# A fused attention and MLP kernel: forward substitution for two groups per instruction, with two layout changes by way of DRAM

## The chip, the cores and the metric

The kernel runs on one core of a Trainium2 chip. The core has a matrix engine (TensorE, PE in the profile), a vector engine (VectorE, DVE), an activation engine (ScalarE, ACT), a general engine (GpSimd, POOL), a sequencer that issues the transfers here (SyncE, SP), and 16 DMA engines between DRAM and the on-chip memory. The metric is the device time of one execution in microseconds (us). The profile is one execution of its own.

## The reference

Three blocks follow each other; the first is a linear attention with a delta rule, the others are MLP blocks. Only the first is touched.

```python
k_n = k / (np.linalg.norm(k, axis=-1, keepdims=True) + 1e-06)
for t in range(S):                       # B, H, S, D = 4, 8, 768, 48
    y[:, :, t] = q[:, :, t] @ state                       # per (b, h)
    v_old = state.T @ k_n[:, :, t]
    state = state + beta[:, :, t] * outer(k_n[:, :, t], v[:, :, t] - v_old)
x = y as (B, S, H * D)                   # 768 tokens of 384 features per batch
x = first MLP(x): gelu(x @ w_in), spatial gate over the tokens, @ w_out, residual
x = second MLP(x): token mixing, then channel mixing, each with a residual
```

## The kernel before

The loop over 768 tokens is cut into chunks of 64 tokens. Inside a chunk the recurrence is a triangular system: with the Gram matrix of the chunk's keys (K Kᵀ), scaled by beta and the norms, its inverse turns values into updates. A 64 x 64 inverse is built from two 32 x 32 blocks, each by forward substitution, and one product that joins them.

The work is staged in **six groups** (two batch pairs, three thirds of the sequence). One group holds 32 blocks of 32 x 32 per 32-row partition quarter. For each group there is a *preparation* and then a *chain*.

The preparation of a group, `prep(g)`:

- Gram blocks: four units of 32 matmuls from Kᵀ (`kq`), each copied out of PSUM by ScalarE in six pieces (L145 to `Md`, L146 to `G`).
- A VectorE transpose of all 32 x 32 blocks (L151) puts the block number on the partitions: `Li`. Then norms and scaling (L155 to L170; L166 scales `Li`).
- The forward substitution: 31 steps. Step j multiplies row j of `Li` with column j of the growing inverse `T` into a scratch tile `p` (L191) and adds it to `T` (L193). A step is split by rows of `T`: rows 0 to 3 and 4 to 11 are two VectorE instructions, the rest one GpSimd instruction, so a step of a late j is six instructions. Every add waits for its product, and every product for the last add.
- Five more VectorE transposes: four (L197) bring the inverse back into the matmul layout `tw`, one (L201) makes `Tn`.
- `merge`: four rounds of 64 small matmuls, each with a ScalarE copy (L209 to L221), join the two halves. `wt`: four units of 32 matmuls with a ScalarE copy (L229, L232).

The masked product of queries and keys, `qk(g)`, has four units; each is masked on VectorE when it leaves PSUM (L128). Gram, `merge`, `wt` and `qk` outputs share two PSUM buffers (`gm`).

The chain of a group, `chain(g)`, goes through its four chunks in 16 *positions*, four per chunk: updates (`ck`, L270), state (`Sps`, L256), outputs (`yp`, L246). It is serial from chunk to chunk. While chain g runs, pieces of later groups are put between its positions by a table (`act`): the preparation of group g+1 is finished, that of group g+2 is begun. So each engine's queue is a fixed order written out by the program; an instruction that waits holds back what is behind it on its engine. SP issues all transfers, in that order too. Dummy matmuls (`wm`, L300) are put between positions to keep PE busy.

Beside chains 0 to 2, the weights `w_in` (64-bit floats) are converted on VectorE, ScalarE and GpSimd in 12 pieces (tile `F`, L413 to L418), and stored to DRAM (`scr`). Beside chain 5 the MLP blocks begin; they run until the end.

## Time and profile before

| | us |
|---|---|
| median of 3 runs (lowest, highest) | 1008.41 (1006.48, 1009.87) |
| span of the profiled execution | 1010.4 |
| PE busy | 889.8 (88 %) |
| DVE busy | 660.8 (65 %) |
| ACT busy | 425.5 (42 %) |
| POOL busy | 317.1 (31 %) |
| DMA | 60.99 MB, mean 60 GB/s |

The profiled execution is 2.0 us longer than the median of the runs. The busy times are unions over the whole span; the attention (up to about 369 us) and the MLP blocks (from about 326 us) have different limits, and must be read apart. A line such as `L191 DVE ... x348 | 87.7, 285 | 1.1` is a group of instructions: 348 of them, 87.7 us busy together, 285 ns on average, and 1.1 us that the engine sat idle just before them. In the table by windows each engine has its busy time and, in brackets, its instructions; then come the granted PE clock (1.00 is full), the share of the 16 DMA engines that was busy, and GB/s. In the timeline the columns are start and duration in us.

### The profile page before, as it was taken

What the parts mean: (1) busy time and instruction counts of PE and PEld (TensorE: products, weight loads), DVE (VectorE), ACT (ScalarE), POOL (GpSimd) and SP (SyncE); (2) the same over time, 40 slices, a digit from 0 to 9 for tenths busy, and PEclk for the clock granted to TensorE, in tenths of its full rate; (3) what the DMA queues carried; (4) which work ended last, traced back from release to release, by engine and by line L of the source; (5) the groups of instructions that cost most, each with busy time, mean ns of one, the idle gap of its engine ahead of it and who ended that gap; (6) DMA issues with size and microseconds to landing.
All of it is one profiled execution on the core that took longest, in us unless ns stands there. A gap on an engine that the chain in (4) does not pass through costs nothing.

```text
span 1010.4 us, 23691 instructions
## 1 busy us (share of the span) xinstructions
PE 889.8 (88%) x9764; PEld 819.7 (81%) x9764; DVE 660.8 (65%) x1612; ACT 425.5 (42%) x1029; POOL 317.1 (31%) x475
## 2 busy tenths in 40 slices
...
GB/s 371 130 49 1 69 127 159 180 57 121 35 75 38 139 125 64 1 1 1 1 2 1 1 72 66 94 63 111 67 24 25 1 24 24 1 24 24 1 25 23
DMA packets 28955, 60.99 MB, mean 60 GB/s; under 512 B 3760, under 2 KB 9904, under 8 KB 28080
## 3 DMA queue, kind: packets, MB, share of 16 engines
...
q14 instruction: 31, 0.25, 0.1%
...
## 4 chain that ended last, share of the span: by engine, by line
PE 59%; DVE 28%; ACT 7%; issue 4%; POOL 1%; DVEq 0%; POOLq 0%; ACTq 0%
PE ps L489 18%; PE ps L490 18%; PE ps L491 18%; DVE p L191 6%; DVE T L193 6%; DVE tw L197 3%; DVE F L413 2%; DVE aq L128 2%; DVE F L414 2%; PE wm L300 1%; PE ps L513 1%; DVE F L415 1%; DVE F L418 1%; ACT Md L145 1%; DVE Li L151 1%
## 5 line engine op out<-in xcount | busy, mean ns | idle before, releaser
L581 DVE SCALAR_TENSOR_TENSOR hlo<-ps,hh 128x384 fp32r<-128x384 f32 x96 | 53.5, 557 | 208.9 <-ACT hh L580 208.9
L580 ACT ACTIVATE hh<-ps 128x384 fp32r<-128x384 f32 x96 | 47.2, 492 | 229.8 <-PE ps L491 229.8
L489 PE MATMUL ps<-GU,SB 128*128 128x384 f32 x288 | 98.7, 343 | 0.0
L491 PE MATMUL ps<-GU,SB 128*128 128x384 f32 x288 | 98.4, 342 | 0.0
L490 PE MATMUL ps<-GU,SB 128*128 128x384 f32 x288 | 98.1, 341 | 0.0
L191 DVE TENSOR_TENSOR p<-Li,T 128x31 f32<-128x31 f32 (+28 forms) x348 | 87.7, 285 | 1.1
L193 DVE TENSOR_TENSOR T<-T,p 128x31 f32<-128x31 f32 (+28 forms) x348 | 84.1, 274 | 0.8
L490 PE MATMUL ps<-SB,VHt 128*128 128x384 f32 x192 | 65.8, 343 | 2.3 <-POOL SB L391 2.3
L491 PE MATMUL ps<-VHt,hlo 128*128 128x384 f32 x192 | 65.3, 340 | 1.3 <-DVE hlo L581 1.3
L300 PE MATMUL wm<-dum 128*128 128x512 bf16 x156 | 51.5, 436 | 16.4 <-DVE dum L319 14.8
L489 PE MATMUL ps<-SB,VHt 128*128 128x384 f32 x192 | 65.6, 341 | 0.0
L491 PE MATMUL ps<-SB,VHt 128*128 128x384 f32 x192 | 65.2, 339 | 0.0
L489 PE MATMUL ps<-VHt,hh 128*128 128x384 f32 x192 | 65.0, 338 | 0.0
L490 PE MATMUL ps<-VHt,hh 128*128 128x384 f32 x192 | 64.6, 337 | 0.0
L556 POOL TENSOR_TENSOR q<-q,u 128x384 f32<-128x384 f32 x32 | 36.9, 1159 | 66.5 <-DVE q L555 66.5
L489 PE MATMUL ps<-X,SA 128*128 128x384 f32 x144 | 50.0, 347 | 7.2 <-DVE xn L568 3.2
L490 PEld LDWEIGHTS ps<-GU,SB 128*128 128x128 f32 x288 | 54.9, 191 | 0.6 <-DVE GU L506 0.6
L489 PEld LDWEIGHTS ps<-GU,SB 128*128 128x128 f32 x288 | 55.0, 191 | 0.5 <-DVE GU L506 0.5
L491 PEld LDWEIGHTS ps<-GU,SB 128*128 128x128 f32 x288 | 54.8, 190 | 0.3 <-POOL SB L391 0.3
L191 POOL TENSOR_TENSOR p<-Li,T 128x19 f32<-128x19 f32 (+19 forms) x115 | 41.4, 360 | 35.2 <-DVE T L168 27.1
L229 PE MATMUL gm<-tw,kn 128*48 128x64 f32 x768 | 30.2, 245 | 23.9 <-DVE aq L128 19.7
L490 PE MATMUL ps<-X,SA 128*128 128x384 f32 x144 | 49.3, 343 | 0.0
...
## 6 DMA issues: line engine op xcount, KB each, us to landing
...
v<-in_vn_dram SPq DMA_DIRECT2D x12, 384.0 KB, 4.2
...
aq<-in_qt_dram SPq DMA_DIRECT2D x8, 512.0 KB, 7.7
...
```

Source lines behind the costliest of these rows:

```text
L128: else: nc.vector.tensor_tensor(aq[rr,par].rearrange("p a c x -> p (a c) x"),gp[rr],mask[rr].rearrange("p t x -> p (t x)").unsqueeze(1).to ...
L191: e.tensor_tensor(p,Li[:,j,j+1:].unsqueeze(1).to_broadcast([128,w,n]),T[:,a:a+w,j].unsqueeze(2).to_broadcast([128,w,n]),ALU.mult)
L193: e.tensor_tensor(T[:,a:a+w,j+1:],T[:,a:a+w,j+1:],p,ALU.add)
L197: nc.vector.transpose(out=tw[rr,q//2,:,co:co+32].rearrange("p n i -> p i n"),in_=T[rr].rearrange("p c i -> p i c"))
L229: nc.tensor.matmul(wt[D_[par],2*pair+cc,:],KNs[pb][F_[par],bb,par,2*h+cc,pair,:],tw[F_[par],par,16*bb+8*h+2*pair+cc,:],start=True,stop=True)
L300: for i in range(n): nc.tensor.matmul(t,dum[:,0:128],dum,start=True,stop=True)
L489: nc.tensor.matmul(ps,L[0],Rr[0],start=first,stop=False)
L490: nc.tensor.matmul(ps,L[0],Rr[1],start=False,stop=False)
L491: nc.tensor.matmul(ps,L[1],Rr[0],start=False,stop=last)
L556: nc.gpsimd.tensor_tensor(gt,gt,u2[:,d,t],ALU.mult)
L580: nc.scalar.activation(hi,ps,AF.Relu)
L581: nc.vector.scalar_tensor_tensor(lo,ps,0.0,R(hi),op0=ALU.max,op1=ALU.subtract)
```

## The change

1. **Substitution.** From group 1 on, groups are solved in pairs, (1,2), (3,4) and then (5) alone. `T` and `Li` have a leading index for the two groups, and a step is two VectorE instructions, one product and one add, over both groups and all rows. GpSimd no longer takes part. Group 0 is solved as before.
2. **Gram blocks to `Li` by DRAM.** From group 1 on, ScalarE copies a whole Gram unit at once (`gf`) and SP stores it to a DRAM tile `gd`. Function `li` reads it back as `Li`, in four transfers per group of 32 x 32 runs of 128 bytes each. The lower-left blocks (`G`) are read from `gd` too (`gload`: two such transfers). The VectorE transpose to `Li` is gone for these groups.
3. **Inverses by DRAM.** `T` is stored to a DRAM tile `td`, and `tload` reads it back into `tw`, in four transfers of 32 x 32 runs of 128 bytes. The four VectorE transposes per group are gone; the one to `Tn` stays.
4. **Kᵀ in quarters.** Instead of two whole tiles there are four tiles of one unit. A list (`_jobs`) gives the order of use by Gram and `qk` units; each use issues the load for the fourth use after it. Kᵀ is so read twice per group. The zero halves of `kq`, `aq` and `kn` are set by memsets at the start and no longer loaded.
5. **Order.** The table `act` has a row per group. Its letters: S a step of the substitution sequence (`li`, three preparatory steps, 31 steps, the stores and `Tn`), K a Gram unit, Q a `qk` unit, t `tload`, G `gload`, m a `merge` or `wt` unit, z the zeroing of `tw`, l and x the load and scaling of V, v the first values, c a step of the weight conversion. No dummy matmuls stand between the positions of a chain any more. All four `qk` units of group 0 are masked on VectorE.

```diff
-        KQs=[P1.tile([128,2,2,2,544],F32,name=f"kq{i}") for i in range(2)]
+        KQs=[P1.tile([128,2,512],F32,name=f"kq{i}") for i in range(4)]
+        GD=[PD.tile([128,32,64],F32,name=f"gd{g}") for g in range(6)]
+        TD=[PD.tile([128,32,32],F32,name=f"td{g}") for g in range(6)]
+        def load_kq():
+            kind,g,u=jobs[put[0]]; bp,sc=groups[g]; kq=KQs[put[0]%4]; put[0]+=1
+            for par in range(2):
+                nc.sync.dma_start(kq[H_[par],par],I['kq'][bp,sc][H_[par],u//2,u%2])
...
+        def kk(g):
...
+                    gf=P2.tile([128,8,64],F32,name="gf")
+                    nc.scalar.copy(gf,gp)
+                    nc.sync.dma_start(GD[g][:,u0:u0+8,:],gf)
...
+        def li(gs):
+            for s,g in enumerate(gs):
+                for q in range(4):
+                    r=slice(32*q,32*q+32); co=32*(q%2)
+                    nc.sync.dma_start(Li[r,s],GD[g][r,:,co:co+32].rearrange("i n j -> n i j"))
+                if g>0: nc.sync.dma_start(BT[gs[0]%2][:,s],I['bt'][groups[g]])
...
-            sets=[((nc.vector,nc.gpsimd)[e],a,b_) for e,a,b_ in ((0,0,d0),(0,d0,bd),(1,bd,32)) if a<b_]
+            if g0==0:
+                sets=[((nc.vector,nc.gpsimd)[e],a,b_) for e,a,b_ in ((0,0,d0),(0,d0,bd),(1,bd,32)) if a<b_]
+            else: sets=[(nc.vector,0,32)]
...
-                    e.tensor_tensor(p,Li[:,j,j+1:].unsqueeze(1).to_broadcast([128,w,n]),T[:,a:a+w,j].unsqueeze(2).to_broadcast([128,w,n]),ALU.mult)
+                    e.tensor_tensor(p,Li[:,S,j,j+1:].unsqueeze(2).to_broadcast(for_),T[:,S,a:a+w,j].unsqueeze(3).to_broadcast(for_),ALU.mult)
-                    e.tensor_tensor(T[:,a:a+w,j+1:],T[:,a:a+w,j+1:],p,ALU.add)
+                    e.tensor_tensor(T[:,S,a:a+w,j+1:],T[:,S,a:a+w,j+1:],p,ALU.add)
...
+                for s,g in enumerate(gs): nc.sync.dma_start(TD[g],T[:,s])
+                for s,g in enumerate(gs):
+                    nc.vector.transpose(out=TN[g%2].rearrange("p n c -> p c n"),in_=T[:,s])
+        def tload(g):
+            for q in range(4):
+                rr=slice(32*q,32*q+32); co=32*(q%2)
+                nc.sync.dma_start(tw[rr,q//2,:,co:co+32],TD[g][rr].rearrange("n c i -> c n i"))
+        def gload(g):
+            for q in (0,2):
+                nc.sync.dma_start(G21s[g%2][rr],GD[g][rr,:,32:64])
...
+        S=seqs(solve((1,2)),later((3,4)),later((5,)))
...
+ACT=[['S2','S2 Q','S2 K','S2','S2 Q K','S2 K','S2 K','S2 Q','S K','Q K t G l','K','K','m c x','m c','m2 c','m4 v'],
+     ['z S','S','t G S c','S','S','Q S2','m S2','Q S2','m S2','l Q S2 m K','S2 m K','Q S2 m K','S2 m K x','S2 m','S2 m','S2 v'],
+     ['z S2','S2','S2 c2','S2','S2 c2','Q S2','Q c2','S4 t G','Q','l Q','S','m','m x','m2','m2','m2 v'],
+     ['z S','S','t G','S','Q S2','S2','Q S2','m S2','Q m S2','l m S2','Q m S2','m S2','m S2 x','m S2','m S2','S4 v'],
+     ['z S3','S3','S3','S6 t G','Q','','Q','','Q m','l m','Q m','m','m x','m','m2','v']]
```

How the orders differ, at the three places on which the prediction rests.

VectorE, before: from the last step of group 0's substitution into the preparation of group 1 (`tw` is the inverse in the matmul layout, `Md` the Gram blocks).

```order
L193 TENSOR_TENSOR T<-T,p_635 128x7
L197 STREAM_TRANSPOSE tw_98<-T 32x32x32 x2
L201 STREAM_TRANSPOSE Tn<-T 128x32x32
L197 STREAM_TRANSPOSE tw_98<-T 32x32x32 x2
L151 STREAM_TRANSPOSE Li<-Md 128x1024
L158 TENSOR_SCALAR rc<-sh 128x32
```

VectorE, now: the same place. The two masks of group 0's first `qk` unit stand where the transpose to `Li` stood; then the preparatory steps have 64 columns, and each step of the substitution is one product and one add over both groups, with the later `qk` masks between them.

```order
L209 STREAM_TRANSPOSE tw_100<-T 32x32x32 x2
L128 TENSOR_TENSOR aq_98<-gm,mask 64x512 x2
L172 TENSOR_SCALAR rc<-sh 128x64
...
L201 TENSOR_TENSOR p_174<-Li,T 128x120
L203 TENSOR_TENSOR T<-T,p_174 128x2x2x30
L128 TENSOR_TENSOR aq_98<-gm,mask 64x512 x2
L201 TENSOR_TENSOR p_174<-Li,T 128x174
L203 TENSOR_TENSOR T<-T,p_174 128x2x3x29
```

So nothing on VectorE waited for a transfer there before; now L172 and all behind it stand behind the eight transfers to `Li`.

SP, now: from the end of chain 0 into chain 1. The loads for group 2 (`kn`, `aq`) wait until chain 0 has read its own; behind them stand `Li` of groups 3 and 4, and behind that `tw` and `G` of group 2.

```order
L87 DMA kn_102<-in_kn_dram 64x2x768 x2
L77 DMA aq_98<-in_qt_dram 64x4x512 x2
L159 DMA Li<-gd_121 32x32x32 x4
L160 DMA bt_143<-in_bt_dram 128x32
L159 DMA Li<-gd_122 32x32x32 x4
L160 DMA bt_143<-in_bt_dram 128x32
L226 DMA tw_100<-td_126 32x32x32 x4
L230 DMA G_148<-gd_120 32x32x32 x2
```

SP, before, at the corresponding place (`kq` is Kᵀ, `st` a piece of the weights):

```order
L76 DMA kq_111<-in_kq_dram 64x4x544 x2
L77 DMA bt<-in_bt_dram 128x32
L96 DMA kn_100<-in_kn_dram 64x2x768 x2
L84 DMA aq_96<-in_qt_dram 64x4x512 x2
L402 DMA st<-in_win_dram 128x512 x2
```

Before, SP only brought operands in; now the substitution and the merges of coming groups wait behind these transfers, which go in the order shown.

More of the change, by code (lines that the diff above doesn't have):

```diff
@@ L129, in qk @@
-                yield 'qk'
-        def prep(g):
-            pb=g%2; tw=TWs[pb]
-            Md=P1.tile([128,32,32],F32,name="Md")
-            G21=Gs[g%2]
-            for h in range(2):
-              for bb in range(2):
-                kq=KQs[g%2][:,h,bb]
+                    nc.vector.tensor_tensor(aq[rr,par].rearrange("p a c x -> p (a c) x"),gp[rr],mask[rr].rearrange("p t x -> p (t x)").unsqueeze(1).to_broadcast([64,8,64]),ALU.mult)
+                yield 'qk'
+        def kk(g):
+            Md=TN[0]
+            for u in range(4):
+                h,bb=u//2,u%2; u0=16*bb+8*h
+                kq=take_kq('k',g,u)
@@ L147, in prep @@
-                yield 'kk'
-            Li=P1.tile([128,32,32],F32,name="Li")
-            T=P1.tile([128,32,32],F32,name="T"); TL[0]=T
-            nc.gpsimd.memset(T,0.0)
-            nc.vector.transpose(out=Li,in_=Md.rearrange("p n i -> p i n"))
+                        c_=kq[F_,par,64*n:64*n+64]
+                        nc.tensor.matmul(gp[T_[par],n],c_,c_,start=True,stop=True)
+                load_kq()
+                if g==0:
+                    for r in range(4):
+                        q=slice(32*r,32*r+32)
+                        nc.scalar.copy(Md[q,u0:u0+8,:],gp[q,:,32*(r%2):32*(r%2)+32])
+                        if r%2==0: nc.scalar.copy(G21s[0][q,u0:u0+8,:],gp[q,:,32:64])
+                else:
+                    gf=P2.tile([128,8,64],F32,name="gf")
+                    nc.scalar.copy(gf,gp)
+                    nc.sync.dma_start(GD[g][:,u0:u0+8,:],gf)
@@ new lines, in kk, with solve @@
+                done[g]+=1
+                yield 'kk'
+        done=[0]*6
+        def li(gs):
+            assert all(done[g]==4 for g in gs)
+            for s,g in enumerate(gs):
[3 more added lines that the diff above has]
+                if g>0: nc.sync.dma_start(BT[gs[0]%2][:,s],I['bt'][groups[g]])
+        def solve(gs):
+            m=len(gs); S=slice(0,m); g0=gs[0]; BTs=BT[g0%2]
+            if g0>0: nc.gpsimd.memset(T[:,S],0.0)
+            else: nc.vector.transpose(out=Li[:,0],in_=TN[0].rearrange("p n i -> p i n"))
+            Lf=Li.rearrange("p s i j -> p s (i j)"); Tf=T.rearrange("p s i j -> p s (i j)")
+            n2=Lf[:,S,0:1024:33]
+            nt=lambda n_:P2.tile([128,2,32],F32,name=n_)[:,S]
+            sh,s1,rc,nr,bi,rr2,nn=[nt(x) for x in ('sh','s1','rc','nr','bi','rr2','nn')]
+            nc.scalar.activation(sh,n2,AF.Sqrt)
@@ L255, in ds @@
                     for par in range(2):
-                        nc.tensor.matmul(Sps[bb][D_[par],pair,:],KNs[pb][F_[par],bb,par,c,pair,:],yr[F_[par],pair,par,:],start=(gc==0 and pair==0 and bb==0),stop=True,skip_group_check=True)
+                        nc.tensor.matmul(Sps[bb][D_[par],pair,:],KNs[pb][F_,bb,par,c,pair,:],yr[F_,pair,par,:],start=(gc==0 and pair==0 and bb==0),stop=True,skip_group_check=True)
                 for par in range(2):
```

286 lines of the change are left out of this document (137 added, 149 removed).

## The prediction

> **What bounds the kernel now.** First the page: span, busy times, and the chain of work that ended last, by engine.
>
> ```profile
> span 1010.4 us, 23691 instructions
> PE 889.8 (88%) x9764; PEld 819.7 (81%) x9764; DVE 660.8 (65%) x1612; ACT 425.5 (42%) x1029; POOL 317.1 (31%) x475
> PE 59%; DVE 28%; ACT 7%; issue 4%; POOL 1%; DVEq 0%; POOLq 0%; ACTq 0%
> ```
>
> PE ends most of the chain, but that is an average over two halves. The view by windows separates them.
>
> ```profile
> core 0: us, PE busy (x) PEld busy (x) DVE busy (x) ACT busy (x) POOL busy (x), PEclk, DMA share, GB/s
> 62.00:112.00 50.00, 35.32 (x817) 27.01 (x815) 48.61 (x158) 31.81 (x84) 22.62 (x49) 0.84 0.12 27
> 160.00:217.00 57.00, 39.27 (x939) 33.62 (x939) 56.02 (x164) 33.08 (x92) 30.28 (x59) 0.85 0.48 129
> 270.00:320.00 50.00, 40.00 (x1172) 34.38 (x1164) 38.74 (x117) 32.30 (x84) 22.53 (x42) 0.97 0.29 72
> 730.00:1010.40 280.40, 276.61 (x1587) 274.83 (x1586) 68.83 (x127) 49.01 (x103) 0.00 (x0) 1.00 0.05 18
> ```
>
> In the attention VectorE is busy 97 to 98% of the time; only beside chain 4, with no substitution left, does it fall to 77%. At the end PE alone bounds, and nothing there changes. So I ask one thing: when does chain 5 start? All behind it keeps its length. The timeline of PE gives the first `ck` of chains 0, 1, 2, 3, 4 and 5:
>
> ```profile
> 70.97 0.32 PE L270 MATMUL ck<-yr,tw 128*64 128x48 f32 x2 [2.40 <-ACT yr L238]
> 131.98 0.34 PE L270 MATMUL ck<-yr,tw 128*64 128x48 f32 x1
> 191.72 0.26 PE L270 MATMUL ck<-yr,tw 128*64 128x48 f32 x1
> 243.80 0.34 PE L270 MATMUL ck<-yr,tw 128*64 128x48 f32 x1
> 290.88 0.26 PE L270 MATMUL ck<-yr,tw 128*64 128x48 f32 x1
> 325.88 0.26 PE L270 MATMUL ck<-yr,tw 128*64 128x48 f32 x1
> ```
>
> Chain 5 starts at 325.9. The distances are 61, 60, 52, 47 and 35 us; the last one is what a chain costs when VectorE has almost no substitution.
>
> **What goes.** The groups, by line:
>
> ```profile
> L191 DVE TENSOR_TENSOR p<-Li,T 128x31 f32<-128x31 f32 (+28 forms) x348 | 87.7, 285 | 1.1
> L193 DVE TENSOR_TENSOR T<-T,p 128x31 f32<-128x31 f32 (+28 forms) x348 | 84.1, 274 | 0.8
> L197 DVE STREAM_TRANSPOSE tw<-T 32x1024 f32<-32x1024 f32 x24 | 47.3, 1971 | 0.9
> L201 DVE STREAM_TRANSPOSE Tn<-T 128x1024 f32<-128x1024 f32 x6 | 11.9, 1990 | 0.2
> L128 DVE TENSOR_TENSOR aq<-gm,mask 64x512 f32<-64x512 f32 x40 | 27.6, 689 | 15.0 <-PE gm L121 14.1
> ```
>
> Substitution costs (87.7 + 84.1)/6 = 28.6 us of VectorE per group, the four transposes 7.9. For the new steps I need the price of one dependent instruction with GpSimd silent:
>
> ```profile
> 107.72 0.19 DVE L191 TENSOR_TENSOR p<-Li,T 128x31 f32<-128x31 f32 x1
> 107.95 0.19 DVE L193 TENSOR_TENSOR T<-T,p 128x31 f32<-128x31 f32 x1
> 109.38 0.28 DVE L191 TENSOR_TENSOR p<-Li,T 128x112 f32<-128x112 f32 x1
> 109.69 0.27 DVE L193 TENSOR_TENSOR T<-T,p 128x112 f32<-128x112 f32 x1
> ```
>
> Start to start 0.23 us at 31 elements and 0.31 at 112: 1.0 ns per element and 0.19 fixed. A step j of a pair has 2(j+1)(31-j) elements; over 31 steps, product and add, that is 21,824. So a pair takes 62 x 0.19 + 21.8 x 1.04 = 34 us, 17 per group instead of 28.6. With the transposes, VectorE loses about 20 of its 50 us per group. It no longer bounds a chain by its sum.
>
> **What comes.** Each `li`, `tload` or `gload` transfer has 1,024 runs of 128 bytes, 64 on each DMA engine. Between two chains' starts stand 6 of them, and 8 more (4 for group 5) where a pair is fetched. No row has such a transfer. Two stretches show small packets, the first with 16-byte rows (`gh`), the second mostly with 128-byte rows (`bt`) at the tail of a Kᵀ load:
>
> ```profile
> DMA packets 142, 0.00 MB, mean 5 GB/s; under 512 B 142, under 2 KB 142, under 8 KB 142
> q1 hardware_dynamic: 142, 0.00, 17.5%
> DMA packets 77, 0.02 MB, mean 56 GB/s; under 512 B 70, under 2 KB 70, under 8 KB 77
> q1 hardware_dynamic: 77, 0.02, 40.1%
> ```
>
> Both windows are 0.4 us of 16 engines, 6.4 us. The first gives 1.12 us/142 = 8 ns per packet, the second 2.57/70 = 37 ns at most; with the seven large ones taken off at about 0.1 us each it is 27. Completion packets of a few bytes are among both. I take the middle of 8 and 28, **18 ns**: a transfer then takes p = 64 x 18 ns = 1.15 us. The ends stay for the range.
>
> The Trainium skill ("DMA: Bandwidth & Descriptors", section "Why small descriptors are slow (HBM only)") has a lower price: each packet carries a fixed overhead of about 3 cycles beside one cycle per 32 bytes. By that, an estimate, 128 bytes take 7 cycles of which 4 move data, some 9 ns, and the sum further down would end at 977 us. Of 128-byte packets no row here shows so low a price.
>
> Ahead of the small runs stand the `kn` and `aq` loads of 64 partitions:
>
> ```profile
> 136.00:140.00 4.00, 3.94 (x92) 2.94 (x88) 4.00 (x25) 3.84 (x13) 1.01 (x2) 1.00 1.07 216
> kn<-in_kn_dram SPq DMA_DIRECT2D x8, 384.0 KB, 5.6
> aq<-in_qt_dram SPq DMA_DIRECT2D x8, 512.0 KB, 7.7
> gh<-in_g_dram SPq DMA_DIRECT2D x1, 2.0 KB, 1.6
> ```
>
> Two of each are 1.8 MB; at 216 GB/s they take 8.5 us. `gh` says that even 2 KB need 1.6 us to land; I add 2 us per batch.
>
> **The sum.** Further rows: the end of group 0's substitution (unchanged), the preparatory steps, the conversion pieces, and the last of the old transposes.
>
> ```profile
> 45.48 3.87 DVE L197 STREAM_TRANSPOSE tw<-T 32x1024 f32<-32x1024 f32 x2
> 104.36 0.18 DVE L158 TENSOR_SCALAR rc<-sh 128x32 f32<-128x32 f32 x1 [0.32 <-ACT sh L155]
> 106.35 1.23 DVE L166 SCALAR_TENSOR_TENSOR Li<-Li,bi 128x1024 f32<-128x1024 f32 x1
> 0.00:340.00 340.00, 17.21 (x48) 0.88 0.39 115
> L197 DVE STREAM_TRANSPOSE tw<-T x24: 1898/1974/2039, 45.5 to 304.7; 32x1024 f32<-32x1024 f32 x24
> ```
>
> Preparatory steps take 107.7 - 104.4 = 3.4 us; with the second scaling and 64 columns 5.0, and 0.6 for the square root. A conversion piece is 17.21/12 = 1.43 us. From the last old transpose (306.7) to chain 5 (325.9) it is 19 us, with merges begun around position 7; a position of that stretch costs about 2.4. So from landed `tw` to the next chain I take 15 us where merges begin at position 12, 17 at 11, 21 at 8 and 24 at 7.
>
> - Chain 1: 45.5 + `li`(1,2) 8p + 2, preparation 5.6, substitution 34, five mask pairs that stand between the steps (7.0), `td` stored 5, `tload` and `gload` 6p + 2, merges 15: 116 + 14p = **132** (before 132.0). Chain 0 is held by VectorE here: its `qk` masks stand behind `li`.
> - Chain 3: 7 us ahead of chain 1's start its old operands are free. Loads 8.5, `li`(3,4) 8p + 2, preparation and one conversion step 8.5, substitution up to step 22 with four mask pairs 34, the rest of it 7, conversion 5.7, `Tn` 4, conversion 2.9 and 2.4 on GpSimd, since the stores of `scr` stand ahead of `li`(5) on SP; `li`(5), `tload`(3), `gload`(3) 10p + 2; merges 17: 87 + 18p = 108 after chain 1, **240** (before 243.8). Chain 2 starts inside this, at about 183.
> - Chain 4: operands free 4 us ahead, 8.5 + 6p + 2 + 24: 30.5 + 6p = 37 later, **277** (290.9).
> - Chain 5: 8.5 + 6p + 2 + 21 = 38 later, **316** (325.9).
>
> In one line: chain 5 starts at 265 + 44p. PE idles up to 10 us while it waits for `tw` in four of the chains, and comes back with half its clock:
>
> ```profile
> 88.00:92.00 4.00, 0.00 (x0) 0.00 (x0) 4.00 (x35) 2.01 (x6) 0.16 (x1) 0.99 0.00 0
> 92.00:96.00 4.00, 0.31 (x2) 0.18 (x2) 3.84 (x3) 0.00 (x0) 0.00 (x0) 0.50 0.00 0
> ```
>
> After 4 us of idleness the granted clock is 0.50. The dummy matmuls that bridged such gaps are gone. I add 1 us per chain, 4 in all: 320, a gain of 6 on 1010.4. The profiled run is 2.0 us above the median, so **1003 us**.
>
> Nothing is counted for ScalarE, whose Gram copies shrink from 24 to 4 per group: it was busy 32 of 50 us beside VectorE's 49; without VectorE's cover it would be next behind PE. The double reading of Kᵀ costs nothing as long as it stays off the queue while `li` runs; it is four quarters ahead. The start keeps its length: dummy matmuls and Gram copies of group 0 are as before.
>
> **The rivals.**
>
> 1. *The short runs are cheap.* At 8 ns, as in the row of 16-byte packets, p = 0.51: 265 + 23 + 4 = 292, 34 earlier: **974**. For it speaks that row, against it the 128-byte one. Below that PE's own 35 us per chain would bind.
> 2. *The queue of short runs becomes the bound: slower.* At 28 ns, p = 1.79: 265 + 79 + 4 = 348, 22 later: **1030**. It decides from 20 ns on, where 44p eats the whole gain. For it speaks the 128-byte row as it stands, and SP's order: merges of group 2 stand behind `li` of groups 3 and 4. Against it: its packets shared their engines with large ones.
> 3. *Two groups per instruction don't do what they say.* If wide, strided steps run at the price seen beside GpSimd, the step below with 84 + 147 = 231 elements,
>
> ```profile
> 31.12 0.65 DVE L193 TENSOR_TENSOR T<-T,p 128x84 f32<-128x84 f32 x2
> 31.69 0.65 DVE L191 TENSOR_TENSOR p<-Li,T 128x80 f32<-128x80 f32 x2
> ```
>
> start to start 0.57 us, less 0.19 fixed, is 1.65 ns per element; a pair takes 48 us instead of 34, twice on the path: 27 later than my sum, **1030**. Against it: GpSimd is silent now.
>
> **How the numbers follow.** Chances: forecast 0.37, cheap runs 0.32, queue 0.25, slow steps 0.06. Two runs can be told apart from about 0.3%, 3 us. The forecast's own range is 990 to 1016, more than half of it faster by over 3 us, a fifth within; cheap runs are nearly all faster; the other two slower. Faster 0.37 x 0.55 + 0.32 x 0.95 = 0.50; within 0.11; slower 0.39. The range goes a little beyond the 8 ns and the 28 ns ends: 970 to 1033.
>
> **What would show it.** In the new profile: chain 5's first `ck` near 320, chain 1's near 132; a wide step of 512 elements at 0.72 us start to start; eight `li` transfers landing 11 us after 45.5; PE waiting for `tw` transfers ahead of merges. If chain 1 is at its place and later chains run ahead by more than 10 us each, the runs are cheap. What would make it wrong: steps at another price per element, a run below 10 or above 28 ns, or chains that wait on ScalarE.

## The result, and the profile after

The changed kernel takes 1023.47 us (median of 4 runs, 1022.84 to 1025.81) against 1008.6 before: ratio **1.016**, 95% interval 1.013 to 1.018. It is slower by 1.6%. The prediction was 1003, faster.

The page of the profiled execution first: span, busy times, and the chain that ended last.

```profile
span 1021.0 us, 23045 instructions
PE 863.1 (85%) x9645; PEld 818.1 (80%) x9646; DVE 582.8 (57%) x1187; ACT 392.3 (38%) x919; POOL 255.2 (25%) x285
PE 58%; DVE 10%; ACT 5%; DMA 3%; issue 3%; POOL 2%; SPq 1%; DVEq 0%; POOLq 0%; ACTq 0%
```

VectorE has lost 78 us of work (660.8 to 582.8) and most of its share of the chain (28% to 10%), and yet the span has grown by 10.6 us. The timeline of PE says where: the first `ck` of chains 0 to 5.

```profile
82.38 1.79 PE L304 MATMUL ck<-yr,tw 128*64 128x48 f32 x32 [1.56 <-ACT yr L272]
148.34 2.10 PE L304 MATMUL ck<-yr,tw 128*64 128x48 f32 x31 [1.56 <-ACT yr L272]
201.09 1.79 PE L304 MATMUL ck<-yr,tw 128*64 128x48 f32 x32 [1.31 <-ACT yr L272]
265.14 2.38 PE L304 MATMUL ck<-yr,tw 128*64 128x48 f32 x32 [1.99 <-ACT yr L272]
298.75 2.21 PE L304 MATMUL ck<-yr,tw 128*64 128x48 f32 x32 [2.01 <-ACT yr L272]
339.10 2.15 PE L304 MATMUL ck<-yr,tw 128*64 128x48 f32 x32 [1.34 <-ACT yr L272]
```

Chain 5 starts at 339.1 instead of 325.9, 13.2 late; what follows takes 681.9 us (684.5 before). So the question of the prediction was the right one: when does chain 5 start? The distances are now 66, 53, 64, 34 and 40 us (before 61, 60, 52, 47, 35). The view by windows, one row for a distance, shows that VectorE is no longer what fills them (its columns: the window and its length, the busy time of PE, PE's weight loads, VectorE, ScalarE and GpSimd with their instructions, PE's granted clock, the DMA share, GB/s):

```profile
82.00:148.00 66.00, 43.70 (x1152) 40.92 (x1152) 39.17 (x69) 32.74 (x82) 12.52 (x11) 0.79 0.56 161
148.00:201.00 53.00, 33.38 (x1024) 31.40 (x1024) 34.97 (x66) 29.50 (x77) 12.75 (x15) 0.84 0.73 163
201.00:265.00 64.00, 33.18 (x864) 31.35 (x864) 37.38 (x82) 27.32 (x72) 18.43 (x24) 0.68 0.66 162
265.00:299.00 34.00, 27.66 (x898) 26.12 (x898) 24.34 (x56) 26.57 (x70) 6.88 (x6) 0.95 0.41 95
299.00:339.00 40.00, 29.74 (x896) 28.04 (x894) 7.93 (x12) 25.91 (x68) 3.49 (x5) 0.87 0.46 101
```

VectorE is busy for 39 of 66 us, 35 of 53, 37 of 64, 24 of 34 and 8 of 40. In the three long distances (66, 53 and 64 us) PE is busy for two thirds of the time at most, ScalarE for 56% at most, and the DMA engines for 56 to 73%. Most of the time that was lost lies in waits. The timelines of SP, VectorE, PE and ScalarE show the way of the first two chains (the last row is the same wait for group 5):

```profile
52.05 3.49 SPq L159 DMA_DIRECT2D Li<-gd  x4
56.50 2.88 SPq L159 DMA_DIRECT2D Li<-gd  x4
63.34 0.20 DVE L172 TENSOR_SCALAR rc<-sh 128x64 f32<-128x64 f32 x1 [5.25 <-ACT sh L169]
110.38 1.94 DVE L219 STREAM_TRANSPOSE Tn<-T 128x1024 f32<-128x1024 f32 x1
119.03 4.14 SPq L226 DMA_DIRECT2D tw<-td  x4
128.46 1.92 PE L243 MATMUL gm<-tw,G 128*32 128x32 f32 x64 [5.70 <-DMA G<-gd]
144.19 1.73 SPq L87 DMA_DIRECT2D kn<-in_kn_dram  x2
147.26 8.73 SPq L159 DMA_DIRECT2D Li<-gd  x4
164.39 0.20 DVE L172 TENSOR_SCALAR rc<-sh 128x64 f32<-128x64 f32 x1 [22.52 <-ACT sh L169]
165.38 1.32 PE L304 MATMUL ck<-yr,tw 128*64 128x48 f32 x15 [11.68 <-ACT yr L292]
238.96 0.26 ACT L169 ACTIVATE sh<-Li 128x32 f32<-128x32 f32 x1 [11.17 <-DMA Li<-gd]
```

`Li` of groups 1 and 2 is issued at 52.05 and there at 63; the pair is solved at 110.4; `tw` of group 1 is issued at 119.0, its merges begin at 128.5, chain 1 at 148.3. `Li` of groups 3 and 4 is issued at 147.3 behind `kn` and `aq`, and VectorE waits 22.5 us for it, PE 11.7: the chain's copy `yr` stands behind the square root `sh` on ScalarE, and `sh` reads `Li`. For group 5, at 238.96, the profile names the transfer to `Li` as what ended an 11.2 us wait of `sh`.

When the groups were solved before is as telling. VectorE's timeline of the kernel before shows the first two of the transposes to `tw` that follow the last step of groups 1, 2, 3 and 4:

```profile
92.15 3.83 DVE L197 STREAM_TRANSPOSE tw<-T 32x1024 f32<-32x1024 f32 x2
139.99 4.04 DVE L197 STREAM_TRANSPOSE tw<-T 32x1024 f32<-32x1024 f32 x2
203.44 3.92 DVE L197 STREAM_TRANSPOSE tw<-T 32x1024 f32<-32x1024 f32 x2
249.78 4.07 DVE L197 STREAM_TRANSPOSE tw<-T 32x1024 f32<-32x1024 f32 x2
```

The pairs are solved at 110.4 and, as VectorE's timeline shows, at 219.8. So groups 1 and 3 are solved 18 and 16 us later than before, and chains 1 and 3 start 16 and 21 us later. Groups 2 and 4 are solved 30 us earlier, and their chains start later all the same.

### The profile page after: what moved, and what is told of

Same layout as the page of the kernel before. It is cut to its first block, busy times and chain, and to the rows that moved or that the text cites. A ratio compares the mean times of both kernels' runs of the same rounds, so it can differ in the third digit from the quotient of the medians.

```text
span 1021.0 us, 23045 instructions
## 1 busy us (share of the span) xinstructions
PE 863.1 (85%) x9645; PEld 818.1 (80%) x9646; DVE 582.8 (57%) x1187; ACT 392.3 (38%) x919; POOL 255.2 (25%) x285
## 4 chain that ended last, share of the span: by engine, by line
PE 58%; DVE 10%; ACT 5%; DMA 3%; issue 3%; POOL 2%; SPq 1%; DVEq 0%; POOLq 0%; ACTq 0%
PE ps L515 17%; PE ps L516 17%; PE ps L517 17%; DVE F L439 2%; DVE F L440 2%; PE ps L539 1%; DVE F L441 1%; PE ck L304 1%; ACT tw L266 1%; DMA aq<-in_qt_dram 1%; PE gm L124 1%; DMA scr<-sh 1%; ACT yr L272 1%; DVE F L444 1%; PE yp L280 1%
## 5 line engine op out<-in xcount | busy, mean ns | idle before, releaser
L304 PE MATMUL ck<-yr,tw 128*64 128x48 f32 x768 | 37.5, 242 | 43.8 <-ACT yr L292 33.4
L304 PEld LDWEIGHTS ck<-yr,tw 128*64 128x64 f32 x768 | 32.3, 154 | 48.0 <-ACT yr L292 34.3
L201 DVE TENSOR_TENSOR p<-Li,T 128x112 f32<-128x112 f32 (+32 forms) x151 | 60.1, 410 | 3.1
L203 DVE TENSOR_TENSOR T<-T,p 128x112 f32<-128x112 f32 (+32 forms) x151 | 59.0, 403 | 3.3
L84 POOL TENSOR_TENSOR v<-v,nn 128x768 f32<-128x768 f32 x12 | 18.0, 1515 | 166.0 <-DMA v<-in_vn_dram 166.0
L128 DVE TENSOR_TENSOR aq<-gm,mask 64x512 f32<-64x512 f32 x48 | 33.1, 689 | 42.9 <-PE gm L124 42.0
L140 PE MATMUL gm<-kq 128*64 128x64 f32 x768 | 32.7, 248 | 28.9 <-ACT gf L149 13.5
L515 PE MATMUL ps<-X,SA 128*128 128x384 f32 x144 | 49.5, 344 | 7.5 <-DVE xn L594 3.1
L140 PEld LDWEIGHTS gm<-kq 128*64 128x64 f32 x768 | 29.8, 161 | 31.7 <-ACT gf L149 14.4
L516 PEld LDWEIGHTS ps<-GU,SB 128*128 128x128 f32 x288 | 54.2, 188 | 0.8 <-DVE GU L532 0.8
L515 PEld LDWEIGHTS ps<-GU,SB 128*128 128x128 f32 x288 | 54.2, 188 | 0.6 <-DVE GU L532 0.6
```

The lines of the kernel that those rows point to most:

```text
L128: nc.vector.tensor_tensor(aq[rr,par].rearrange("p a c x -> p (a c) x"),gp[rr],mask[rr].rearrange("p t x -> p (t x)").unsqueeze(1).to_broad ...
L140: nc.tensor.matmul(gp[T_[par],n],c_,c_,start=True,stop=True)
L201: e.tensor_tensor(p,Li[:,S,j,j+1:].unsqueeze(2).to_broadcast(for_),T[:,S,a:a+w,j].unsqueeze(3).to_broadcast(for_),ALU.mult)
L203: e.tensor_tensor(T[:,S,a:a+w,j+1:],T[:,S,a:a+w,j+1:],p,ALU.add)
L304: nc.tensor.matmul(u2[T_[par],pair,:],tw[F_,par,16*bb+8*h+2*pair+cc,:],yr[F_,pair,par,:],start=True,stop=True)
L515: nc.tensor.matmul(ps,L[0],Rr[0],start=first,stop=False)
```

## The experiments

All are compared with the kernel before, run on the same chip beside them. Chips differ (the kernel before took 1008.6 us beside the changed kernel, 1004.9 beside e16 and e17), so a difference between two runs is given here as the difference of their ratios times 1008.6 us. The starts are read from PE's timeline as above; they are those of the one profiled execution, which lies up to 4.4 us off the median of its run (e5's is the fastest of its four, e7's the slowest).

| run | ratio to before (95%) | chain 1 | chain 3 | chain 5 |
|---|---|---|---|---|
| before | 1 | 132.0 | 243.8 | 325.9 |
| changed | 1.016 (1.013 to 1.018) | 148.3 | 265.1 | 339.1 |
| e1 root off ScalarE | 1.025 (1.022 to 1.028) | 147.9 | 269.8 | 343.9 |
| e2 `tw` first | 1.032 (1.027 to 1.037) | 148.9 | 277.1 | 351.4 |
| e3 both | 1.032 (1.029 to 1.034) | 150.0 | 280.9 | 355.2 |
| e4 Gram before dummies | 1.017 (1.015 to 1.018) | 147.5 | 262.8 | 336.8 |
| e5 `Li` of 3, 4 early | 1.013 (1.010 to 1.017) | 154.7 | 262.2 | 334.8 |
| e6 and first steps | 1.016 (1.014 to 1.018) | 150.3 | 270.8 | 341.2 |
| e7 `tw` by VectorE | 1.010 (1.007 to 1.013) | 146.9 | 271.8 | 340.2 |
| e8 long runs | 1.010 (1.007 to 1.012) | 146.2 | 260.7 | 334.9 |
| e16 third `gf` | 1.020 (1.017 to 1.023) | 149.9 | 265.3 | 339.4 |
| e9 new order | 1.023 (1.019 to 1.026) | 154.0 | 262.7 | 345.6 |
| e10 and start | 1.026 (1.023 to 1.029) | 155.9 | 263.8 | 348.8 |
| e17 pairs, reordered | 1.010 (1.006 to 1.013) | 151.4 | 248.4 | 329.2 |
| e11 no pairs | 1.002 (0.999 to 1.004) | 135.6 | 242.0 | 327.2 |
| e15 no pairs, 1 held | 1.021 (1.017 to 1.025) | 154.3 | 258.2 | 342.5 |
| e12 no pairs, start | 1.011 (1.007 to 1.015) | 147.4 | 253.4 | 337.1 |
| **e13 no pairs, reordered** | **0.988 (0.984 to 0.992)** | 130.9 | 232.5 | 311.7 |
| e14 and Gram first | 0.989 (0.985 to 0.993) | 130.9 | 231.8 | 311.2 |

### Which wait? One at a time, in the changed kernel

**e1.**

```diff
-            nc.scalar.activation(sh,n2,AF.Sqrt)
+            if g0>0: nc.vector.tensor_scalar(sh,n2,0.5,0.5,ALU.mult,ALU.add)
```

> Edit: for groups 1 to 5 the square root sh of the pair's diagonal is not an instruction of ScalarE but one tensor_scalar of VectorE of the same 128x64 tile, (n2+1)/2, the first Newton step from 1; the exact root is left out, nothing else changes. So ScalarE never waits for the Li transfers. Theory A (ScalarE's queue): the changed kernel loses its time because sh waits for Li on ScalarE, in order, and the copies XZ and yr of the chain stand behind it; TensorE's waits for ScalarE of 11.7 us (chain 1) and 10.5 us (chain 2), which end with a late sh, vanish and chain 5 starts 15 to 22 us earlier than 339: 1002 to 1009 us. Theory B (SyncE's queue): the tw and G transfers of the next group are issued late, behind Li, scr and Kt loads; then TensorE only waits further on, for tw and G at its merges, and the gain is under 5 us: 1018 to 1023. Chain 0 stays near 82 by both, since the masks of its QK blocks stand on VectorE behind the same Li transfers.

1032.6 us. **e2** (rows of the table; `t` and `G` issue `tw` and `G`):

```diff
-['S2',...,'S K','Q K t G l',...   ['z S','S','t G S c',...   ['z S2',...,'S2 c2','Q S2','Q c2','S4 t G',...
+['S2',...,'S t G K','Q K l',...   ['z t G S','S','S c',...   ['z S2',...,'S2 t G c2','Q S2','Q c2','S4',...
```

> Edit: only places in the table of the order. The tw and G transfers of groups 1, 2 and 3 are issued one to three positions earlier: group 2's ahead of Li of groups 3 and 4, group 3's right behind td and ahead of the scr stores and Li of group 5, group 1's ahead of two Kt loads and two Gram stores. Theory B (SyncE's queue): chain 1 starts 3 to 5 us earlier, chain 2 some 3, chain 3 some 10, in all 13 to 18 us at chain 5: 1005 to 1011 us. Theory A (ScalarE's queue): Li of groups 3 and 4 now lands about 5 us later, sh waits that much longer and the yr copies of chain 1 with it; the gain of chain 1 is given back, chain 2 is still held by sh and by the squares of the conversion: 1018 to 1025.

1036.4 us. **e3** is both edits:

> Edit: both together, root off ScalarE and tw, G first. Theory A: as the root alone, 1002 to 1009. Theory B: as the order alone, 1005 to 1011. If either wait only hides the other, the two together gain clearly more than the sum of the two alone, with chain 5 some 25 us earlier: about 998.

1039.5 us. Theory A and theory B both fall: e1 and e2 each took away a wait that its theory named, and all three runs are slower than the changed kernel, by 9, 16 and 16 us. PE's timeline in e1:

```profile
171.26 2.08 PE L244 MATMUL gm<-tw,G 128*32 128x32 f32 x64 [9.89 <-DMA G<-gd]
```

The timelines of VectorE and PE in e2:

```profile
172.31 0.20 DVE L172 TENSOR_SCALAR rc<-sh 128x64 f32<-128x64 f32 x1 [29.05 <-ACT sh L169]
173.31 1.32 PE L304 MATMUL ck<-yr,tw 128*64 128x48 f32 x15 [19.79 <-ACT yr L292]
```

In e1 PE has lost its 11.7 us for `yr` and waits 9.9 for `G` instead. In e2 `tw` and `G` are early, `Li` of 3 and 4 lands 8 us later for it, and the 11.7 are 19.8. Why e1 costs as much as 9 us isn't shown. **e4** puts the dummy matmuls, which PE runs from 41.2 to 49.1 ahead of the last Gram unit, behind it:

```diff
-            if ns==cfg.get('wj',18): ...warm(cfg.get('wu',24))
+            if ns==cfg.get('wj',22): ...warm(cfg.get('wu',24))
```

> Edit: the 24 dummy matmuls of 7.9 us, which start at 41.2, are put behind the last Gram quarter of group 2 instead of ahead of it (one number: step 22 instead of 18). Then its copy, its store and the Li transfers behind it on SyncE start at about 43.5 instead of 52.1. Expected by both theories: sh at 55 instead of 63, chain 0 at 74 to 76 instead of 82.4, all later chains shifted with it: 6 to 8 us less, 1015 to 1017. If chain 0 is held by something else (kn, merges), under 2 us.

1024.0 us, no difference. `Li` was issued 3.7 us earlier, but in this execution group 0 was solved 1.8 later (48.55 instead of 46.73); chain 1 starts 0.9 earlier. **e5** and **e6** move `Li` of 3 and 4 into chain 0:

```diff
-'m c x','m c','m2 c','m4 v'],
+'S m c x','m c','m2 c','m4 v'],          (e5)
+'S m x','m','m2 S','m4 S2 v c3'],        (e6)
```

> Edit: only the table of the order. The step that issues the Li transfers of groups 3 and 4 moves from chain 1's position 0, where it stands on SyncE behind the kn and aq loads that wait for the end of chain 0, to chain 0's position 12, ahead of the conversion; all later steps of the substitution stand one step earlier. Theory C: after chain 1 the time is set by the way Li(3,4), substitution of 3 and 4, td, tw, merges, chain 3, and this way begins late, since SyncE holds those transfers until 147 while VectorE idles from 117 to 164. Then Li lands near 141, sh runs at chain 1's position 0 near 150 instead of 164, substitution ends 13 us earlier, chain 3 starts near 252 instead of 265: 1008 to 1012 us, and TensorE's wait of 11.7 us in chain 1 is gone. Theory B (tw and G hold the chains): gain under 4 us.

> Edit: as before, and the preparation and first step of the substitution of groups 3 and 4 (three steps more) also move into chain 0's last two positions; the conversion pieces that stood at its positions 12 to 14 move behind them. Theory C: sh at 143, substitution ends near 199, chain 3 near 246: 1001 to 1006 us. Theory B: no more than the run with the transfers alone.

1021.6 and 1024.5 us: theory C falls too. In e5 the eight transfers push the loads `st` of the conversion back; its squares wait for them on ScalarE, and the merge's copy `XZ` behind these (PE waits 10.1 us, chain 1 starts 6.4 later). In e6 the pair 3, 4 is solved 6.4 us earlier, at 213.4 instead of 219.8, but SP takes it back. The timelines of VectorE and SP in e6, where the first row is the transpose that ends the pair:

```profile
213.36 3.65 DVE L219 STREAM_TRANSPOSE Tn<-T 128x1024 f32<-128x1024 f32 x2
242.32 3.02 SPq L226 DMA_DIRECT2D tw<-td  x4
```

29 us from solved to `tw`: `scr` stores, loads of `st`, `Li` of group 5 and Kᵀ loads stand ahead on SP. **e7** undoes the inverses' way through DRAM:

```diff
-                nc.sync.dma_start(tw[rr,q//2,:,co:co+32],TD[g][rr].rearrange("n c i -> c n i"))
+                nc.vector.transpose(out=tw[rr,q//2,:,co:co+32].rearrange("p n i -> p i n"),in_=T[rr,(g-1)%2].rearrange("p c i -> p i c"))
```

> Edit: one part of the change undone. The inverses of groups 1 to 5 get into tw by four transposes of VectorE per group again (7.9 us), not by the store td and four transfers of 128-byte runs; Li and G still go through DRAM, substitution stays two groups wide. The transposes stand at chain 0's position 9, chain 1's 0, chain 2's 4, chain 3's 2, chain 4's 3. If td and tw are on the path (theory B): merges of group 1 begin at 125 instead of 128.5, those of group 3 near 232 instead of 245, chain 5 starts 10 to 16 us earlier: 1007 to 1013 us. By theory C chain 1 gains 3, chain 3 some 10, since the transposes follow the substitution at once: near 1010 too, but Li(3,4) still lands at 164 and the wait of 11.7 us stays. If VectorE's 40 us more are what counts: slower than 1023.

1019.7 us, 5.5 less than the changed kernel, about half of the least that either theory expected. PE now waits 16.2 us for the `yr` behind the square root of group 5. **e8** takes the short runs away from `Li`:

```diff
-                    nc.sync.dma_start(Li[r,s],GD[g][r,:,co:co+32].rearrange("i n j -> n i j"))
+                    nc.sync.dma_start(Li[r,s],GX[r])
```

> Edit: the 20 Li transfers read a constant tile in DRAM (128 partitions, one run of 4 KB each, stored there at the start) instead of the Gram blocks in runs of 128 bytes; bytes, count and place stay. The Gram blocks' way into Li is left out, so the inverses are those of constant blocks. At the measured 14 ns per run (4,565 packets in the 4 us from 57 to 61), eight transfers take 7.2 us; in long runs at 216 to 400 GB/s 2.6 to 4.9. Theory C (order, not price): 2 to 5 us less per pair, 1 to 2 for group 5, in all 4 to 10 us: 1013 to 1019. The prediction's second rival (the queue of short runs is the bound, 28 ns each): the eight would lose 9 to 12 us, in all 20 or more: below 1003.

1018.1 us, 6 less: as by theory C, the order, and not by the second rival. The runs have a price, but not one that decides. **e16** gives ScalarE a third buffer for Gram copies:

```diff
-                    gf=P2.tile([128,8,64],F32,name="gf")
+                    gf=P2.tile([128,8,64],F32,name="gf",bufs=3)
```

> Edit: the changed kernel with three buffers gf for the Gram copies instead of two, nothing else. ScalarE waits 26.6 us in it for the landing of Gram stores. If these waits hold the chains: 3 to 6 us less, 1018 to 1020. If they lie beside VectorE's substitution (chain 0) and beside other waits: no difference over 3 us.

1026.1 us, 4 more than the changed kernel with intervals that overlap: no gain.

### Or the whole order?

**e9** rewrites the table. A letter `u` issues `tw` and `G` of group g+2 in chain g; the other letters are as told above.

```diff
+                    if a=='u': zero(g+2); tload(g+2); gload(g+2)
-ACT=[[...,'S K','Q K t G l','K','K','m c x','m c','m2 c','m4 v'], ['z S','S','t G S c',...
+ACT=[[...,'S t G K c','Q K l','K','K c','S m x','u m c','m2 S','m4 S2 v'], ['S2 m','S2 m','S2 m K','S2 m',...
```

> Edit: all operations, transfers and sizes of the changed kernel stay; only the table of the order is rewritten, with one new letter that issues tw, G and the zeroing of group g+2 at chain g's position 13 or 14. tw of the parity that a chain has used is free after its last ck (position 12), but the changed kernel issues the next tw only behind the next chain's kn, aq and Li. So tw, G of groups 2, 4 and 5 come 15 to 25 us earlier and their merges stand in the first four positions of the chain ahead; Li of 3 and 4 stands at chain 0's position 12; Li of 5 and its root stand behind the substitution of 3 and 4. Theory D (order: merges wait in each chain for transfers that could have been issued a chain's end earlier, and each fix alone only moves the wait): chain 1 near 146, chain 2 near 186 (was 201), chain 3 near 225 (265), chain 4 near 261 (299), chain 5 near 297 (339): 975 to 990 us. Theory E (the work of TensorE and ScalarE in a chain, with two shared buffers between them, bounds it at 50 us whatever the order): within 5 us of the changed kernel.

**e10** also puts merges and masks of group 0 ahead of the pair's first steps:

```diff
-        many(S,1)
-        for k_ in range(4): many(m0,1); many(qks[0],1); ...many(S,cfg.get('s1',2))
+        for k_ in range(4): many(m0,1); many(qks[0],1)
+        many(S,3); scale_v(0)
```

> Edit: as before, and at the start the merges and masks of group 0 are put ahead of the first steps of groups 1 and 2 on VectorE and ScalarE, and the dummy matmuls behind the last Gram quarter. Chain 0 then starts near 72 instead of 82, and the substitution of 1 and 2 ends some 4 us earlier, because five masks are out of its way and Li lands earlier. By theory D chain 1 starts near 141 and all behind it 4 to 6 us earlier than in the run before: 970 to 985 us.

1030.2 and 1032.3 us: theory D falls in this form, and so does theory E's "within 5 us" by a little. In e10 chain 0 does start early, at 73.98, and chain 1 not before 155.9: the pair that feeds it is solved at 111.6, as late as ever, and the way from there to chain 1 has grown from 38 us to 44. My own table also had a fault: in e9 it put `Li` of group 5 ahead of `tw` of group 3 on SP (213.8 and 223.9).

### The pairing alone

**e11** solves one group per instruction, on VectorE, through DRAM; a group takes its own half of `Li` and `T` in turn:

```diff
-            m=len(gs); S=slice(0,m); g0=gs[0]; BTs=BT[g0%2]
+            m=len(gs); g0=gs[0]; S=slice(g0%2,g0%2+1); BTs=BT[g0%2]
-        S=seqs(solve((1,2)),later((3,4)),later((5,)))
+        S=seqs(*(solve((g,)) for g in range(1,6))); Ls=[3,4,5]
```

> Edit: the pairing alone is undone: one group per instruction, still on VectorE alone, Li, tw and G still through DRAM; Li and T keep their two halves, used in turn, so that the Li transfers of group g+2 are issued as soon as group g is solved. The table of the order is written anew for that (one group's 35 steps per chain, tw and G of group g+2 at chain g's position 14 where they are solved by then). VectorE's substitution costs 23 us per group instead of 17. Theory F (latency of the pair): in the changed kernel group 1 is ready only when group 2 is, 47 us after Li has landed, and eight transfers instead of four stand ahead of it; saved VectorE time is not what the chains wait for. Then group 1 is solved near 91 instead of 110, chain 1 starts near 122 to 130 instead of 148, and each chain follows after 36 to 42 us: chain 5 at 275 to 300, 960 to 985 us. Theory E (a chain costs 50 us whatever feeds it): chain 1 near 130, chain 5 near 320, 1000 to 1008. If VectorE's work is the bound: 30 us more of it, slower than 1023.

1009.2 us: 14 us less than the changed kernel, level with the kernel before. The timelines of VectorE, SP and PE:

```profile
94.67 1.99 DVE L220 STREAM_TRANSPOSE Tn<-T 128x1024 f32<-128x1024 f32 x1
99.01 3.15 SPq L227 DMA_DIRECT2D tw<-td  x4
135.64 1.79 PE L305 MATMUL ck<-yr,tw 128*64 128x48 f32 x32 [1.70 <-ACT yr L273]
327.16 1.79 PE L305 MATMUL ck<-yr,tw 128*64 128x48 f32 x32 [0.95 <-ACT yr L273]
```

Group 1 is solved at 94.7 instead of 110.4, chain 1 starts 12.7 earlier, chain 5 11.9. Theory F had expected far more, 960 to 985 us: it had the later chains follow after 36 to 42 us, and they follow after 51, 55, 45 and 40. And the order of e11 is new too. So **e15** changes one thing in e11: `tw`, `G` and merges of group 1 wait until group 2 is solved.

```diff
-'S2 Q t G L',...,'S5 m x','S5 m','S5 m2 c','S5 m4 v u L'],
+'S2 Q L',...,'S5 x','S5','S5 c','S5 t G m8 v u L'],
```

> Edit: one position in the run with one group per instruction that took 1009: tw, G and merges of group 1 are held until group 2 is solved too (position 15 of chain 0 instead of 7, the eight merge steps there too), as a pair makes them wait; nothing else changes. Theory F: group 2 is solved some 34 us behind group 1, so chain 1 starts 12 to 20 us later, and the whole is 10 to 18 us slower: 1019 to 1027, the time of the changed kernel. If the latency of the first pair is not what costs, under 5 us.

The timelines of SP and PE in e15:

```profile
128.92 3.17 SPq L227 DMA_DIRECT2D tw<-td  x4
137.05 1.92 PE L244 MATMUL gm<-tw,G 128*32 128x32 f32 x64 [21.10 <-DMA G<-gd]
154.29 1.79 PE L305 MATMUL ck<-yr,tw 128*64 128x48 f32 x32 [1.70 <-ACT yr L273]
342.50 2.14 PE L305 MATMUL ck<-yr,tw 128*64 128x48 f32 x32 [1.03 <-ACT yr L273]
```

1027.2 us, 19 more, a little above what theory F expected: chain 1 starts 18.7 later and chain 5 still 15.3. So most of what is lost there doesn't come back. (It holds the group longer than a pair does, to 128.5 instead of 110.4, so it shows that such a delay counts, not how much a pair costs.) **e12** is e11 with e10's start:

> Edit: as before, and at the start merges and masks of group 0 stand ahead of the first steps of group 1, the dummy matmuls behind the last Gram quarter. Theory F: chain 0 near 72, group 1 solved some 3 us earlier, the whole 2 to 6 us less than in the run before. If chain 1 is set by tw of group 1 alone, no difference over 3 us.

1018.9 us, 10 worse. Group 1's root now stands behind group 0's merges on ScalarE, and the group is solved at 103.0 instead of 94.7. Chain 0 starts at 78.8, close to e11's 77.2, so this run tells little about chain 0; that group 1 is solved 8.3 later fits the loss.

### A version that beats both, and the pairs with its order

**e13** takes down the waits that e11's profile showed, one by one:

```diff
-                    gf=P2.tile([128,8,64],F32,name="gf")
+                    gf=P2.tile([128,8,64],F32,name="gf",bufs=4)
...
+ACT=[['S2','S2 Q','S2 K','S2','S2 Q K','S2 K','S2 K','S2 Q','S3 K t G','S4 Q K l','S4 K','S4 K c','S5 m x','S5 m','S5 m2 L','S5 m4 v'],
+     ['S3','S3 c','S3 z t G K','S3','S3 K','S3 m','S3 m K c','S3 m Q','S3 m Q K','S4 l Q','S4 m Q','m c L','m x','m','u','v'],
...
+     ['','','','m','m','m','m Q','Q','Q','l Q','m','m','m x','m','','v']]
```

> Edit: the run with one group per instruction, its waits taken down one by one, with the same operations. Four buffers gf instead of two, so that a Gram copy on ScalarE need not wait 12 us for the landing of the store before last, with chain 1's merges behind it; Li of the next group is issued in the middle of a chain, not ahead of kn and aq; QK blocks stand at positions 6 to 10, behind the landing of aq (TensorE stood 7 to 9 us at position 4 in three chains); tw two to three positions behind td. Theory F (latency, waits in order): chain 1 5 to 8 us earlier, chains 2 to 4 3 to 6 us each: 990 to 1000 us. Theory E (a chain costs what it costs): within 4 us of 1009.

> Edit: as before, and the dummy matmuls behind the last Gram quarter at the start. Li of group 1 lands 3 to 5 us earlier. If the path starts with that landing: 3 us less than the run before; if the masks and merges of group 0 on VectorE set it, no difference.

994.6 and 996.1 us: e13 is faster than before by 1.2% (interval of the ratio 0.984 to 0.992), as theory F expected this time; the Gram unit first (e14) adds nothing. The page of e13 first (busy times, shares of the chain, and one group of instructions):

```profile
PE 868.4 (87%) x9646; PEld 823.5 (83%) x9646; DVE 614.2 (62%) x1331; ACT 392.8 (39%) x921; POOL 250.4 (25%) x287
PE 62%; DVE 21%; ACT 5%; issue 4%; DMA 3%; SPq 3%; POOL 2%; DVEq 0%; POOLq 0%; ACTq 0%
L202 DVE TENSOR_TENSOR p<-Li,T 128x31 f32<-128x31 f32 (+28 forms) x213 | 73.1, 352 | 5.1
```

And PE's timeline of e13, the starts of chains 1 and 5:

```profile
130.91 1.79 PE L305 MATMUL ck<-yr,tw 128*64 128x48 f32 x32 [1.70 <-ACT yr L273]
311.74 1.79 PE L305 MATMUL ck<-yr,tw 128*64 128x48 f32 x32 [0.95 <-ACT yr L273]
```

VectorE works 31 us more than in the changed kernel (614.2 and 582.8), and the kernel is 28 us faster. Which of e13's edits gains what was not tried one by one. **e17** gives the pairs an order by the same rules, with a third `gf` (two of the five rows):

```diff
...
+     ['S2','S2 c','S2','S2 m K','S2 m','S2 m K','S2 m K c','S2 Q','S2 Q K','S2 l Q','S2 m Q','S2 m','S2 m x c','S3 m','S4','v'],
+     ['','z t G c','','','m','m','m c','m Q','Q S','l Q','m Q','m c','m x','m','u','v'],
...
```

> Edit: the pairs kept, with the order that served best without them: three buffers gf; tw and G of groups 2, 4 and 5 at chain positions 13 and 14 of the chain before; QK blocks at positions 7 to 10; Li of 5 in the middle of chain 2, its substitution wholly in chain 3. Theory F (the pair's latency): chain 1 stays near 148 and chain 3 waits for the pair 3, 4, so this stays 10 to 20 us above the 995 of the run without pairs: 1005 to 1015. If the order alone was at fault: within 4 us of 995.

1015.8 us: 6 less than the changed kernel, 22 more than e13; chain 1 starts 20.5 later than in e13, chain 5 17.5. That is what theory F expected, or a little more; that the order alone was at fault falls. So of the 28 us between the changed kernel and e13 some 22 go with the pairs and 6 with the order. The split holds for these two tables; that no other order serves the pairs better isn't shown. One thing is the same in all runs: with pairs group 1 is solved at 109 to 113 us, without them at 94 to 103, and chain 1 starts 34 to 45 us behind that (60 in e15, which holds it back).

## Why the prediction was wrong

**What held.** VectorE stopped bounding the attention. A wide step costs what was predicted, 0.73 us start to start at 512 elements (0.72), and the substitution's two lines (products, adds) now take 60.1 and 59.0 us in all, before 87.7 and 84.1. VectorE's timeline of the changed kernel, a product and its add:

```profile
89.35 0.69 DVE L201 TENSOR_TENSOR p<-Li,T 128x512 f32<-128x512 f32 x1
90.08 0.69 DVE L203 TENSOR_TENSOR T<-T,p 128x512 f32<-128x512 f32 x1
```

Its page, the same two lines:

```profile
L201 DVE TENSOR_TENSOR p<-Li,T 128x112 f32<-128x112 f32 (+32 forms) x151 | 60.1, 410 | 3.1
L203 DVE TENSOR_TENSOR T<-T,p 128x112 f32<-128x112 f32 (+32 forms) x151 | 59.0, 403 | 3.3
```

A pair takes 41.9 us (68.48 to 110.34), less five mask pairs of 1.42: 34.8, predicted 34. `Li` landed 11 us after its issue, as predicted. The third rival (1.65 ns per element) is out.

**The price of a run.** The DMA view of the changed kernel from 57 to 61 us, in which only short runs move (packets, bytes, and how many of them are small):

```profile
DMA packets 4565, 0.57 MB, mean 143 GB/s; under 512 B 4565, under 2 KB 4565, under 8 KB 4565
```

4.00 us of 16 engines, 64 us, over 4,565 runs: at most **14 ns**, below the 18 taken, and below the 20 from which the second rival was to decide. So that rival, with its 1030 us, came out near the measured time by luck: with 14 ns its own sum gives 265 + 44 x 0.90 + 4 = 309, a gain of 17 us, and long runs in the place of all of `Li`'s short ones (e8) save 6. The forecast's 18 ns were too dear as well, and hid 11 us of what follows. The estimate from the Trainium skill ("DMA: Bandwidth & Descriptors", "Why small descriptors are slow (HBM only)"), some 9 ns, is too low for these runs. The first rival's 8 ns are out as well.

**What failed is the handovers in the sum.** A handover here is the way from one engine's result to the engine that needs it: issue, landing, copy. With the run at 14 ns, chain 5 should have started at 309 and did at 339. Term by term:

- *"45.5 ... `li`(1,2)"*: the transfers were issued at 52.05, behind the dummy matmuls and the last Gram unit; 6.6 us. The start kept its length to 1.3 us (group 0 is solved at 46.7 instead of 45.5). But chain 0, of which the sum said only that it is held behind `li`, starts at 82.4 instead of 71.0, its masks on VectorE and its `XZ` on ScalarE behind the wait for `Li`. Issuing `Li` 3.7 us earlier (e4) brought chain 1 forward by only 0.9.
- *"`td` stored 5, `tload` and `gload` 6p + 2"*: from 110.4 to 128.5 it was 18.1 instead of 12.4. `tw` was issued 8.6 us behind `td`: eight Kᵀ loads and two Gram stores stood between them on SP. The double reading of Kᵀ was said to cost nothing as long as it stays off the queue while `li` runs; here it stood ahead of `tw`.
- *"merges 15"*: 19.9; for chain 3 18.9 instead of 17.
- *Chain 3, "loads 8.5, `li`(3,4) 8p + 2"*: 15.7 instead of 10.7 behind chain 1's start; then 12.5 us from solved to the issue of `Li`(5) instead of 9.3, and 14.0 from there to the first merge instead of 11. PE came to that merge without a wait for `tw`, since `yr` had held it until 239.6.
- Predicted stretches in which VectorE works (5.6 + 34 + 7 ahead of chain 1, 55.2 ahead of chain 3) came to 47.4 and 55.7. The last two distances were 2 us shorter and 3 longer than the sum; the 4 us for PE's clock can't be told from the waits.

Ahead of chain 1 the misses with the landing of `Li` (1.8) and VectorE (0.8) make 19.8, ahead of chain 3 13.6. As far as the timelines show, all of them but 3 us lie in the handovers: transfers issued late on SP, and merges that wait for their copies and for their place between the chain's own work.

**Why that turned the sign.** The sum had the pair's 34 us on the way to chain 1, at the right price, so the pair isn't the term that failed. By the sum the pair was solved at about 103 (45.5 + 11.2 + 5.6 + 41), 11 us later than group 1 before (92.15). It still had chain 1 at 132.0, as before, because it set 29 us from there to the chain (5 + 8.9 + 15). Before, that way took 39.8 us, and now it takes 38.0: the 15 us for merges came from the stretch ahead of chain 5, the transfers were priced without the queue ahead of them, and the way from solved to chain did not get shorter.

**What the sum didn't ask.** Ahead of chain 1 only group 1 is wanted. Alone it takes 23.6 us of substitution (e11, 63.96 to 94.63 less five mask pairs), the pair 34.8, and four more transfers stand ahead of the pair. The pair's latency is on the path, and the time that it saves VectorE is not: e11, e15 and e17 show that, with the limits said there. "Nothing is counted for ScalarE" was wrong too in that ScalarE's order holds the chain behind `sh` (two waits of PE, of 11.7 and 10.5 us; a third, of 10.7, is behind the conversion's squares, which the profile shows waiting for VectorE's part of the conversion); but e1 shows that removing `sh` alone gains nothing, since `G` was not there either.
